# Decoding the signs of 64-bit weights with a Prelu activation, taking arithmetic off GpSimd, and a list ordered anew

## The chip, the cores and the metric

One Trainium2 chip, one of its cores. The metric is the device time of the whole program in microseconds (us), median over runs. The engines are TensorE (PE in the profile, PEld for its weight loads), VectorE (DVE), ScalarE (ACT), GpSimd (POOL) and SyncE (SP), which issues the transfers.

## What is computed

Attention with a learned bias on positions, followed by a two-layer feed-forward block on all tokens (4 batches x 576 positions, 8 heads of 64, model width 512, hidden width 2048):

```python
scores = scale * np.matmul(q, k.transpose(0, 1, 3, 2))
x = (psi_rel / psi_i)[..., None]
h = np.maximum(x @ w1 + b1, 0.0)
bias = h @ w2
scores = scores + bias.transpose(2, 0, 1)[None, :, :, :]
scores = scores - np.max(scores, axis=-1, keepdims=True)
attn = np.exp(scores)
attn = attn / (np.sum(attn, axis=-1, keepdims=True) + 1e-09)
return np.matmul(attn, v).astype(np.float32)
...
x = np.ascontiguousarray(attn_out.transpose(0, 2, 1, 3)).reshape(B * S, H * D)
...
h = x @ w_in
g = h - np.tanh(h)
return (g @ w_out).astype(np.float32)
```

The two weight matrices arrive as 64-bit floats (512x2048 and 2048x512), everything else as 32-bit floats.

## The kernel before, in words

All matrix products run in 16-bit types with every operand split into a high and a low part ("h" and "l", line 403 makes the low one by a subtraction), and three or four products are summed for one.

The program has these steps. Every one is an operation in a list; buffers are named by step.

- Bias: 36 groups of 16 positions. Four ReLU passes (`hg`, 128x576, line 448 on ScalarE or 450 on VectorE), a product with `w2` (`pb`, line 460), a scaled copy out (`bo`, line 469 or 470), and a store to a table in device memory (`bias_d`). The tables `bt` are loaded from there.
- Keys and values: 16 tiles `kv` (128x1152), loaded (`kvst`), narrowed to the high part (line 384 or 385), low part by line 529, and a small rearrangement on GpSimd (lines 536 to 538).
- Weights: 16 chunks `wi` and 16 chunks `wo` of 128x512 (function `weight_chunk`). Each chunk is loaded as pairs of 32-bit words and turned into a 32-bit float: line 489 shifts the low word right by 29, line 494 puts the sign bit of the high word into it, line 384, 385 or 387 multiplies the high word by 2^-111 as a float, line 502 shifts it left by 3 and joins the low word. Then it is narrowed (`win_hi`, `wout_h`) and the low part subtracted (`win_lo`, `wout_l`).
- Attention: 10 blocks (group of two batches, 128 or 64 query rows), in each four pairs of heads. Scores (`ps`, line 588), bias and row minimum (line 602, VectorE), exponential (line 616, ScalarE), reciprocal (623, 624), high part (384, ScalarE), low part (632, VectorE), a transposing transfer (`pt`, line 642, SyncE), product with the values (`px`, line 664), copies `xt` (394, 682).
- Feed-forward, some way behind the attention: `ph` (line 703), tanh (715), h - tanh(h) (720), high part `gh` (384), low part `gl` (402 or 403), `po` (line 730), copies `ot` (394, 395) and the store.

The order is not written by hand. `Plan.order` is a list scheduler that runs through the program once with a duration per operation (`c_mm`, `c_dve`, `c_act` and so on), a latency from each engine to the next (`LAT`), a modelled transfer queue, and a priority per operation (a formula plus a correction from the table `ADJ`). At each moment each free engine takes the ready operation with the best priority. An operation may name several engines (`narrow`, `minus`, `WAYS`); it goes to the one that is done first by weighted load. What comes out is a fixed order on every engine; on the chip each engine takes its own list strictly from the top, and waits by semaphores.

Of the kernel before, what the change touches and what calls it, by code (L numbers as in the profile page):

```python
# [61 lines left out]
class Op:  # L62
    __slots__ = ("alts", "eng", "cost", "fn", "prio", "deps", "outs", "bufs", "start", "end", "left", "idx", "ready", "port")
# [5 lines left out]
class Plan:  # L69
    LAT = {"pe": 190.0, "dve": 200.0, "act": 60.0, "pool": 60.0, "dma": 0.0}  # L70
# [52 lines left out]
    def op(self, eng, cost=None, fn=None, r=(), w=(), prio=0.0, psum=False):  # L123
# [5 lines left out]
        o.port = {e for e, c, _ in alts if e == "pool" and not isinstance(c, tuple) or e == "dve" and not psum}  # L129
# [29 lines left out]
    def order(self):  # L159
# [17 lines left out]
        while done < len(self.ops):  # L177
            moved = False
            claims = {} if loose else self.claimed(cand, now, slots, limit)
            for e in free:  # L180
# [3 lines left out]
                for o in cand[e]:  # L184
                    if o.ready > now or port > now and e in o.port:
                        continue
                    if best is not None and (o.prio, o.idx) >= (best.prio, best.idx):
                        continue
                    if len(o.alts) > 1:
                        mine = now + self.load(e, o.alts[e][0])  # L190
                        if any(
                            max(free[x], now, port if x in o.port else 0.0) + self.load(x, a[0]) < mine
                            for x, a in o.alts.items()
                            if x != e
                        ):
                            continue
# [23 lines left out]
                if isinstance(o.cost, tuple):  # L220
                    issue, move, after, hold = o.cost
                    if e == "dma":
                        hw = max(hw, now) + issue
                        begin = max(hw + 650.0, xfer)
                    else:
                        begin = max(now + SWDGE_HOLD + 650.0, xfer)
# [75 lines left out]
def kernel(  # L302
# [78 lines left out]
    def narrow(n, out, in_, scale=1.0, ptr=0, kind="moe"):  # L381
# [3 lines left out]
            "pool": ("pool", c_pool(n, ptr), lambda: G.tensor_scalar(  # L385
                out(), in_(), scale() if ptr else scale, 1.0, ALU.mult, ALU.mult)),
# [19 lines left out]
    def move(nbytes, out, in_, r=(), w=(), prio=0.0, part=P, hold=(), soft=False):  # L406
# [10 lines left out]
        c = c_dma(nbytes, part)  # L417
# [16 lines left out]
    def bias_group(t, prio):  # L434
# [5 lines left out]
        for j in range(4):  # L440
# [16 lines left out]
        def mms():  # L457
# [7 lines left out]
        op("pe", 1000, mms, r=[(h, y) for h in hgs for y in range(2)] + ["w2"], w=[pb], prio=prio)  # L465
# [10 lines left out]


    def weight_chunk(src, hi, lo, key, prio):
# [3 lines left out]
        def words(i, dt=F32):  # L482
# [10 lines left out]
            "dve", c_dve2(512),  # L493
            lambda: V.scalar_tensor_tensor(  # L494
# [388 lines left out]
```

## Time and profile before

| what | value |
|---|---|
| runs | 680.49, 682.80 and 682.97 us, median 682.8 |
| the profiled execution | span 679.7 us, first to last instruction; what lies around the span is not recorded, the median of the runs is 3.1 us longer |
| busy: PE, DVE, ACT, POOL | 609.4, 485.8, 422.9, 72.2 us |
| mean granted clock of PE | 0.962 of full speed |
| DMA | 114.24 MB, mean 168 GB/s |
| chain that ended last | PE 77%, DVE 15%, DMA 4%, ACT 2%, issue 2% |

Shares are of the span. PE's busy time counts from the first to the last moment at which a matmul is in flight, so it says when PE had work, not how fast it was. In timelines an operation's recorded time overlaps that of the next on its engine by some 0.09 us, so what an operation costs its engine is read from start to start.

### The profile page before, as it was taken

What the parts mean: (1) busy time and instruction counts of PE and PEld (TensorE: products, weight loads), DVE (VectorE), ACT (ScalarE), POOL (GpSimd) and SP (SyncE); (2) the same over time, 40 slices, a digit from 0 to 9 for tenths busy, and PEclk for the clock granted to TensorE, in tenths of its full rate; (3) what the DMA queues carried; (4) which work ended last, traced back from release to release, by engine and by line L of the source; (5) the groups of instructions that cost most, each with busy time, mean ns of one, the idle gap of its engine ahead of it and who ended that gap; (6) DMA issues with size and microseconds to landing.
All of it is one profiled execution on the core that took longest, in us unless ns stands there. A gap on an engine that the chain in (4) does not pass through costs nothing.

```text
span 679.7 us, 18908 instructions
## 1 busy us (share of the span) xinstructions
PE 609.4 (90%) x8096; PEld 481.8 (71%) x8096; DVE 485.8 (71%) x1001; ACT 422.9 (62%) x778; POOL 72.2 (11%) x98
## 2 busy tenths in 40 slices
PE   1782546986999999999999999999999999999997
PEld 0221224764787778788888888888888888888897
DVE  4999999799877867677777987677687576433231
ACT  4996667588776667566665767565587575432231
POOL 4400022010100100000111502000010000000000
PEclk9887677998999999999999999999999999999999
DMA  8898886886755887599968799777578379240010
GB/s 315 291 327 304 222 235 109 275 220 140 264 101 121 155 241 115 135 238 196 240 151 219 164 199 180 165 182 156 90 150 213 71 144 209 41 92 2 1 33 17
DMA packets 193779, 114.24 MB, mean 168 GB/s; under 512 B 171152, under 2 KB 176416, under 8 KB 193696
## 3 DMA queue, kind: packets, MB, share of 16 engines
q1 hardware_dynamic: 193632, 113.03, 68.4%
q8 instruction: 63, 1.03, 0.6%
q14 instruction: 20, 0.16, 0.1%
q0 software_dynamic: 64, 0.02, 0.1%
HBM read 55.22 MB, written 15.34 MB: 104 GB/s over the span
## 4 chain that ended last, share of the span: by engine, by line
PE 77%; DVE 15%; DMA 4%; ACT 2%; issue 2%; SPq 0%; ACTq 0%; DVEq 0%
PE ph L703 28%; PE po L730 28%; PE ps L588 11%; PE px L664 8%; PE pb L460 3%; DVE hl L632 2%; DVE s L602 2%; DMA bt<-bias_d 2%; DMA kvst<-kv 1%; DVE hg L450 1%; DVE ws_wo L494 1%; DVE ws_wo L502 1%; DVE bo L470 1%; DVE ws_wi L502 1%; DMA ws_wi<-w_in 1%
## 5 line engine op out<-in xcount | busy, mean ns | idle before, releaser
L703 PE MATMUL ph<-xt,win_hi 128*128 128x256 f16 (+1 forms) x1280 | 193.8, 262 | 2.7 <-DVE xt L682 1.6
L730 PE MATMUL po<-gh,wout_l 128*128 128x256 bf16 (+1 forms) x640 | 162.3, 263 | 1.0 <-DVE wout_l L403 1.0
L730 PE MATMUL po<-gh,wout_h 128*128 128x256 bf16 (+1 forms) x640 | 162.7, 263 | 0.0
L730 PE MATMUL po<-gl,wout_h 128*128 128x256 f16 (+1 forms) x640 | 162.3, 263 | 0.1
L703 PE MATMUL ph<-xt,win_lo 128*128 128x256 f16 (+1 forms) x640 | 161.4, 262 | 0.4 <-DVE win_lo L403 0.4
L616 ACT ACTIVATE s<-s,mx 128x576 f32<-128x576 f32 x144 | 110.7, 769 | 70.2 <-DVE mx L602 69.6
L703 PEld LDWEIGHTS <-win_hi 128*128 128x128 f16 x1280 | 116.6, 98 | 22.3 <-issue 11.3
L730 PEld LDWEIGHTS <-wout_h 128*128 128x128 f16 x1280 | 117.9, 98 | 19.6 <-issue 8.2
L632 DVE SCALAR_TENSOR_TENSOR hl<-s,mx,hl 128x576 f16<-128x576 f32 x144 | 118.3, 854 | 9.4 <-ACT hl L384 9.2
L588 PE MATMUL ps<-kv,qq 64*128 64x288 f16 (+1 forms) x1280 | 91.8, 304 | 27.9 <-DVE mx L602 15.3
L602 DVE CUSTOM_DVE_ANT_0 s<-ps,bt 128x576 f32<-128x576 f32 x144 | 105.0, 752 | 16.4 <-PE ps L588 15.1
L384 ACT ACTIVATE hl<-s,mx 128x576 f16<-128x576 f32 x144 | 104.3, 764 | 8.1 <-issue 3.1
L720 DVE SCALAR_TENSOR_TENSOR tt<-tt,ph 128x512 f32<-128x512 f32 x72 | 49.4, 687 | 80.1 <-ACT tt L715 80.0
L715 ACT ACTIVATE tt<-ph 128x512 f32<-128x512 f32 x72 | 42.9, 596 | 89.4 <-PE ph L703 89.0
L460 PE MATMUL pb<-hg,w2s 128*32 128x288 f32 x576 | 68.1, 453 | 33.7 <-ACT hg L448 23.2
L588 PEld LDWEIGHTS <-qq 64*128 64x128 f16 (+1 forms) x1280 | 56.0, 103 | 55.5 <-issue 27.6
L460 PEld LDWEIGHTS pb<-hg,w2s 128*32 128x32 f32 x576 | 23.2, 114 | 70.9 <-ACT hg L448 44.5
L664 PEld LDWEIGHTS <-kv 128*64 128x64 f16 x2400 | 63.5, 112 | 10.2 <-issue 10.0
L664 PE MATMUL px<-pt,kv 128*64 128x128 f16 (+1 forms) x2400 | 69.0, 217 | 0.6 <-DMA pt<-hl 0.6
L703 PEld LDWEIGHTS <-win_lo 128*128 128x128 f16 x640 | 62.6, 98 | 8.1 <-issue 1.8
L730 PEld LDWEIGHTS <-wout_l 128*128 128x128 f16 x640 | 63.0, 98 | 7.2 <-DVE wout_l L403 1.2
L448 ACT ACTIVATE hg<-zt,b1l 128x576 f32<-128x576 f32 x83 | 59.5, 763 | 0.5 <-DVE win_lo L403 0.5
(54 smaller groups left out, 477.5 us busy)
## 6 DMA issues: line engine op xcount, KB each, us to landing
bt<-bias_d SPq DMA_DIRECT2D x32, 576.0 KB, 4.9
bias_d<-bo SPq DMA_DIRECT2D x36, 288.0 KB, 4.0
kvst<-kv SPq DMA_DIRECT2D x16, 576.0 KB, 7.3
ws_wi<-w_in SPq DMA_DIRECT2D x16, 512.0 KB, 6.4
ws_wo<-w_out SPq DMA_DIRECT2D x16, 512.0 KB, 6.4
bt<-bias_d SPq DMA_DIRECT2D x16, 288.0 KB, 6.1
qst<-qF SPq DMA_DIRECT2D x8, 512.0 KB, 4.3
outT<-ot SPq DMA_DIRECT2D x16, 256.0 KB, 4.7
```

The costliest lines, as they stand in the source:

```text
L384: "act": ("act", c_act(n, ptr), lambda: A.activation(out(), in_(), AF.Copy, scale=scale() if ptr else scale)),
L448: lambda to=to, src=src, bs=bs: A.activation(to(), src, AF.Relu, bias=bs, scale=1.0)),
L460: nc.tensor.matmul(pb()[32 * j : 32 * j + 32, x, :HS], w2s, hgs[j // 2]()[:, j % 2, x * HS : x * HS + HS], start=True, stop=True, tile_pos ...
L588: nc.tensor.matmul(pss[j]()[w * e : w * e + w, x, :HS], qq()[dp, a, c0 + w * e : c0 + w * e + w], ks()[dp, y, x * HS : x * HS + HS], start ...
L602: V.tensor_tensor_reduce(s().rearrange("p (x k) -> p x k", x=2), ps()[:, :, :HS], bt()[:, j].rearrange("p (x k) -> p x k", x=2), -0.125 / ...
L616: A.activation(s(), s(), AF.Exp, bias=m()[:, j : j + 1], scale=-1.0, accum_out=m()[:, 2 + j : 3 + j])
L632: V.scalar_tensor_tensor(hl()[:, 1, hs], s(), m()[:, 6 + j : 7 + j], hl()[:, 0, hs], ALU.mult, ALU.subtract)
L664: nc.tensor.matmul(px()[64 * j : 64 * j + 64, w * bb : w * bb + w], kw()[:, y, v : v + 64], pt()[:, NCH * l + c, col : col + w], start=(n ...
L703: nc.tensor.matmul(ph()[:, n * (f - f0) : n * (f - f0) + n], w[:, k, f * P : f * P + P], xs[k]()[:, a, :n], start=(k == 0 and e == 0), sto ...
L715: "act", c_actp(512), lambda ph=ph, tt=tt: A.activation(tt(), ph(), AF.Tanh, scale=1.0 / SH),
L720: lambda ph=ph, tt=tt: V.scalar_tensor_tensor(tt(), tt(), -SH, ph(), ALU.mult, ALU.add),
L730: nc.tensor.matmul(po()[:, d // 2, n * (d % 2) : n * (d % 2) + n], wout[w][:, f, d * P : d * P + P], x()[:, n * (f - f0) : n * (f - f0) + ...
```

## The change

1. In `weight_chunk` the sign step (line 494) and the multiplication after it become one activation: `Prelu` with scale 2^-111 and, for negative words, another factor of 2^32. That factor sets the exponent bit that the shift by 3 moves to the sign's place. The step is ScalarE's alone; the multiplication could go to three engines before.
2. GpSimd loses all arithmetic on tiles (`narrow`, `minus`, the ReLU): narrowing goes to ScalarE or VectorE, subtractions to VectorE. It keeps the rearrangement of `kv`, two small loads and one small multiplication.
3. The durations and latencies of the scheduler are other numbers, the transfer model has another form, and the rule that VectorE and GpSimd exclude each other (`port`) is gone.
4. `ADJ` is another table, with an entry for almost every step. The engines' lists differ throughout.

The lists hold 990 rows for VectorE before and 984 now, for ScalarE 619 and 639, for GpSimd 103 and 60, for SyncE 235 and 232; PE has the same 15186 rows in another order.

```diff
-    LAT = {"pe": 190.0, "dve": 200.0, "act": 60.0, "pool": 60.0, "dma": 0.0}
+    LAT = {"pe": 200.0, "dve": 118.0, "act": 132.0, "pool": 85.0, "dma": 0.0}
...
-                    d.ready = max(d.ready, now + (0.0 if same else lat))
+                    d.ready = max(d.ready, now + (SAME[o.eng] if same else lat))
...
+SAME = {"pe": 0.0, "dve": 60.0, "act": 60.0, "pool": 0.0, "dma": 0.0}
...
 def c_dve2(n, ptr=0):
-    return n * 1.05 + 150.0 + 60.0 * ptr
+    return n * 1.0417 + 70.0 + 60.0 * ptr
...
 def c_act(n, ptr=0):
-    return n * 0.833 + 200.0 + 93.0 * ptr
+    return n * 0.8333 + 105.0 + 82.0 * ptr
...
     def minus(n, out, a, b):
-        return [
-            ("pool", c_pool2(n), lambda: G.tensor_tensor(out(), a(), b(), ALU.subtract)),
-            ("dve", c_dve2(n), lambda: V.tensor_tensor(out(), a(), b(), ALU.subtract)),
-        ]
+        return [("dve", c_dve2(n), lambda: V.tensor_tensor(out(), a(), b(), ALU.subtract))]
...
         op(
-            "dve", c_dve2(512),
-            lambda: V.scalar_tensor_tensor(
-                words(0, U32), words(1, U32), 0x80000000, words(0, U32), ALU.bitwise_and, ALU.bitwise_or
-            ),
-            r=[(st, 1)], w=[(st, 0)], prio=prio,
+            "act", c_act(512) + 40.0,
+            lambda: A.activation(words(1), words(1), AF.Prelu, scale=2.0 ** -111, alpha=2.0 ** 32),
+            w=[(st, 1)], prio=prio,
         )
-        op(narrow(512, lambda: words(1), lambda: words(1), 2.0 ** -111, kind="w"), w=[(st, 1)], prio=prio)
...
-    "kv": ("act", "pool"),
-    "w": ("act", "pool", "dve"),
-    "q": ("act", "pool"),
+    "kv": ("act", "dve"),
+    "w": ("act", "dve"),
+    "q": ("act", "dve"),
...
-ADJ = {"wo60": -2.382, "wo00": 1.592, "wo130": 0.423, "wi21": 0.943,
+ADJ = {"b0": 1.041, "b1": -1.377, "b10": -0.125, "b11": -0.096, "b12": 1.001,
```

Three places show how the lists moved. In a name, the last number tells buffers of one kind apart and means nothing else.

**VectorE, the first weight chunk** (`ws_wi_0`, from its first shift to its low part). Before:

```order
L489 TENSOR_SCALAR ws_wi_0_134<-ws_wi_0_134 128x512
L450 TENSOR_SCALAR hg_192<-zt,b1l 128x576
L494 SCALAR_TENSOR_TENSOR ws_wi_0_134<-ws_wi_0_134 128x512
L450 TENSOR_SCALAR hg_205<-zt,b1l 128x576
L387 TENSOR_SCALAR ws_wi_0_134<-ws_wi_0_134 128x512
L489 TENSOR_SCALAR ws_wi_0_150<-ws_wi_0_150 128x512
L502 SCALAR_TENSOR_TENSOR ws_wi_0_134<-ws_wi_0_134 128x512
L470 TENSOR_SCALAR bo_225<-pb_211,rls 128x576
L387 TENSOR_SCALAR win_hi<-ws_wi_0_134 128x512
L494 SCALAR_TENSOR_TENSOR ws_wi_0_150<-ws_wi_0_150 128x512
L403 TENSOR_TENSOR win_lo<-ws_wi_0_134,win_hi 128x512
```

Now:

```order
L477 TENSOR_SCALAR ws_wi_0_137<-ws_wi_0_137 128x512
L440 TENSOR_SCALAR hg_195<-zt,b1l 128x576
L458 TENSOR_SCALAR bo_201<-pb_183,rls 128x576
L487 SCALAR_TENSOR_TENSOR ws_wi_0_137<-ws_wi_0_137 128x512
L440 TENSOR_SCALAR hg_209<-zt,b1l 128x576
L440 TENSOR_SCALAR hg_222<-zt,b1l 128x576 x2
L394 TENSOR_TENSOR win_lo<-ws_wi_0_137,win_hi 128x512
```

The sign step (L494) and the scaling (L387) between shift (L489, now L477) and join (L502, now L487) are gone from VectorE, and the chunk's narrowing (`win_hi`) has moved to ScalarE here.

**ScalarE, at the same chunks** (among the ReLU passes `hg` and the copies `bo` of the bias groups). Before:

```order
L469 ACTIVATE bo_208<-pb_195,rls 128x576
L448 ACTIVATE hg_223<-zt,b1l 128x576 x2
L448 ACTIVATE hg_232<-zt,b1l 128x576 x2
L384 ACTIVATE ws_wi_0_150<-ws_wi_0_150 128x512
L448 ACTIVATE hg_251<-zt,b1l 128x576
L469 ACTIVATE bo_255<-pb_241,rls 128x576
L384 ACTIVATE win_hi<-ws_wi_0_150 128x512
```

Now:

```order
L438 ACTIVATE hg_159<-zt,b1l 128x576
L482 ACTIVATE ws_wi_0_137<-ws_wi_0_137 128x512
L438 ACTIVATE hg_195<-zt,b1l 128x576
L438 ACTIVATE hg_199<-zt,b1l 128x576 x2
L438 ACTIVATE hg_209<-zt,b1l 128x576
L379 ACTIVATE win_hi<-ws_wi_0_137 128x512
L482 ACTIVATE ws_wi_0_157<-ws_wi_0_157 128x512
```

The Prelu (L482) stands in ScalarE's list for each chunk, ahead of the join on VectorE, and the narrowing behind it.

**VectorE, just ahead of the first bias-and-minimum of the third attention block** (the row `s_1_0_0_0`; `tt` and `gl` belong to the feed-forward of the second block, `ot` to the first block's output). Before:

```order
L502 SCALAR_TENSOR_TENSOR ws_wo_0_1853<-ws_wo_0_1853 128x512
L450 TENSOR_SCALAR hg_2250<-zt,b1l 128x576
L682 SCALAR_TENSOR_TENSOR xt_0_3_2237<-px_3_2145,xt_0_3_2237 128x256
L470 TENSOR_SCALAR bo_2256<-pb_2239,rls 128x576
L450 TENSOR_SCALAR hg_2284<-zt,b1l 128x576
L450 TENSOR_SCALAR hg_2289<-zt,b1l 128x576 x2
L403 TENSOR_TENSOR qq_2_2208<-qst_2_2209,qq_2_2208 128x1024
L720 SCALAR_TENSOR_TENSOR tt_0_2304<-tt_0_2304,ph_0_2258 128x512
L450 TENSOR_SCALAR hg_2360<-zt,b1l 128x576 x2
L403 TENSOR_TENSOR gl_0_2366<-tt_0_2304,gh_0_2358 128x512
L395 TENSOR_SCALAR ot_1_2388<-po_1454 128x256
L602 ISA s_1_0_0_0_2418,mx_1_0_0_2419<-ps_0_1_0_0_2368,bt_1_0_2212 128x576
```

Now:

```order
L487 SCALAR_TENSOR_TENSOR ws_wo_0_2085<-ws_wo_0_2085 128x512
L705 SCALAR_TENSOR_TENSOR tt_0_2259<-tt_0_2259,ph_0_2190 128x512
L394 TENSOR_TENSOR wout_l<-ws_wo_0_2079,wout_h 128x512
L394 TENSOR_TENSOR wout_l<-ws_wo_0_2085,wout_h 128x512
L394 TENSOR_TENSOR gl_0_2283<-tt_0_2259,gh_0_2269 128x512
L705 SCALAR_TENSOR_TENSOR tt_2_2281<-tt_2_2281,ph_2_2227 128x512
L440 TENSOR_SCALAR hg_2337<-zt,b1l 128x576 x2
L394 TENSOR_TENSOR gl_2_2345<-tt_2_2281,gh_2_2339 128x512
L440 TENSOR_SCALAR hg_2343<-zt,b1l 128x576
L440 TENSOR_SCALAR hg_2348<-zt,b1l 128x576
L587 ISA s_1_0_0_0_2400,mx_1_0_0_2401<-ps_0_1_0_0_2350,bt_1_0_2252 128x576
```

Ahead of this row stand 316 rows before and 290 now. The last weight chunks stand closer to it, and the second hidden group of that feed-forward (`tt_2`, `gl_2`) has come ahead of it.

## Rows read from the trace of the kernel before

**Rows 1.** Six stretches: length, busy PE, PEld, DVE, ACT, POOL (instructions), PEclk, DMA share, GB/s

```profile
0.00:12.00 12.00, 0.00 (x0) 0.00 (x0) 2.62 (x3) 2.65 (x3) 3.43 (x9) 1.00 0.77 274
12.00:62.00 50.00, 31.96 (x192) 9.67 (x192) 48.68 (x87) 43.30 (x62) 12.16 (x24) 0.89 0.94 331
62.00:120.00 58.00, 31.54 (x474) 18.19 (x475) 54.96 (x116) 39.49 (x74) 9.83 (x9) 0.68 0.75 187
120.00:184.60 64.60, 55.29 (x911) 41.96 (x911) 57.26 (x119) 49.10 (x85) 8.25 (x9) 0.97 0.80 230
184.60:610.00 425.40, 425.40 (x5552) 351.58 (x5553) 303.66 (x650) 271.83 (x527) 38.53 (x48) 1.00 0.74 159
610.00:680.00 70.00, 65.24 (x980) 60.39 (x974) 18.67 (x30) 16.52 (x30) 0.00 (x0) 0.99 0.05 14
```

**Rows 2.** Waits of PE over the whole run: us in total, times, longest

```profile
PE pb L460 <- ACT hg L448: 23.2, 12, 13.7
PE ps L588 <- DVE mx L602: 15.3, 7, 4.7
PE ps L588 <- ACT qq L384: 9.6, 1, 9.6
```

**Rows 3.** Waits of PE from 184.6 us to the end, all there are

```profile
PE ph L703 <- DVE tt L720: 0.4, 1, 0.4
```

**Rows 4.** Timeline of DVE (start, us): first bias-and-minimum of the third attention block

```profile
184.61 0.76 DVE L602 CUSTOM_DVE_ANT_0 s<-ps,bt 128x576 f32<-128x576 f32 x1 [0.24 <-PE ps L588]
```

**Rows 5.** Timeline of DVE, 166 to 172 us

```profile
166.80 0.94 DVE L450 TENSOR_SCALAR hg<-zt,b1l 128x576 f32<-128x576 f32 x2
167.66 0.45 DVE L387 TENSOR_SCALAR wout_h<-ws_wo 128x512 f16<-128x512 f32 x1
168.02 0.45 DVE L489 TENSOR_SCALAR ws_wo<-ws_wo 128x512 uint32<-128x512 uint32 x1
168.36 0.70 DVE L403 TENSOR_TENSOR wout_l<-ws_wo,wout_h 128x512 f16<-128x512 f32 x1
168.99 0.67 DVE L494 SCALAR_TENSOR_TENSOR ws_wo<-ws_wo 128x512 uint32<-128x512 uint32 x1
169.59 1.53 DVE L470 TENSOR_SCALAR bo<-pb,rls 128x576 f32<-128x576 f32 x2
171.04 0.67 DVE L502 SCALAR_TENSOR_TENSOR ws_wo<-ws_wo 128x512 uint32<-128x512 uint32 x1
```

**Rows 6.** Chain of waits in order of time: one feed-forward group, one bias group

```profile
191.11 2.62 PE ph L703 x24
210.67 1.11 PE pb L460 x16
```

**Rows 7.** Waits of DVE in the first 180 us

```profile
DVE kv L529 <- POOL kv L385: 3.4, 1, 3.4
DVE ws_wi L502 <- ACT ws_wi L384: 0.6, 1, 0.6
DVE ws_wo L502 <- ACT ws_wo L384: 0.4, 1, 0.4
```

**Rows 8.** DVE in the first 180 us, groups by line: the attention's low part

```profile
L632 DVE SCALAR_TENSOR_TENSOR hl<-s,mx,hl 128x576 f16<-128x576 f32 x24 | 21.0, 913 | 0.0
```

**Rows 9.** The same operation over the whole run: ns min/median/max

```profile
L632 DVE SCALAR_TENSOR_TENSOR hl<-s,mx,hl x144: 797/814/1714, 77.7 to 601.9; 128x576 f16<-128x576 f32 x144
```

**Rows 10.** Timeline of ACT, 60 to 63 us

```profile
61.45 0.68 ACT L384 ACTIVATE ws_wo<-ws_wo 128x512 f32<-128x512 f32 x1
62.04 0.61 ACT L384 ACTIVATE qq<-qst 128x512 f16<-128x512 f32 x1
```

**Rows 11.** ACT in the first 180 us, groups by line

```profile
L384 ACT ACT_TABLE_LOAD x1 | 1.3, 1283 | 0.7 <-PEq L872 0.7
L384 ACT ACTIVATE ws_wi<-ws_wi 128x512 f32<-128x512 f32 x10 | 6.8, 679 | 2.4 <-issue 1.7 <-DVE ws_wi L494 0.6
```

**Rows 12.** POOL from 180 us on, costliest group

```profile
L402 POOL TENSOR_TENSOR gl<-tt,gh 128x512 f16<-128x512 f32 x13 | 16.1, 1238 | 254.9 <-ACT gh L384 254.8
```

More of the change, by code (lines that the diff above doesn't have):

```diff
@@ L62 @@
 class Op:
-    __slots__ = ("alts", "eng", "cost", "fn", "prio", "deps", "outs", "bufs", "start", "end", "left", "idx", "ready", "port")
+    __slots__ = ("alts", "eng", "cost", "fn", "prio", "deps", "outs", "bufs", "start", "end", "left", "idx", "ready")
 SWDGE_HOLD = 1040.0
 class Plan:
-    LAT = {"pe": 190.0, "dve": 200.0, "act": 60.0, "pool": 60.0, "dma": 0.0}
+    LAT = {"pe": 200.0, "dve": 118.0, "act": 132.0, "pool": 85.0, "dma": 0.0}
     def __init__(self):
@@ L121, in claimed, with op @@
         return claims
-    def op(self, eng, cost=None, fn=None, r=(), w=(), prio=0.0, psum=False):
+    def op(self, eng, cost=None, fn=None, r=(), w=(), prio=0.0):
         o = Op()
         alts = eng if isinstance(eng, list) else [(eng, cost, fn)]
-        o.port = {e for e, c, _ in alts if e == "pool" and not isinstance(c, tuple) or e == "dve" and not psum}
         o.alts = {e: (c, f) for e, c, f in alts}
@@ L184, in order @@
                 for o in cand[e]:
-                    if o.ready > now or port > now and e in o.port:
+                    if o.ready > now:
                         continue
@@ L191, in order @@
                         if any(
-                            max(free[x], now, port if x in o.port else 0.0) + self.load(x, a[0]) < mine
+                            max(free[x], now) + self.load(x, a[0]) < mine
                             for x, a in o.alts.items()
@@ L220, in order @@
                 if isinstance(o.cost, tuple):
[L221 to L226, printed above, removed]
+                    issue, lead, move, after, hold = o.cost
+                    begin = max(now + (lead if e == "dma" else SWDGE_HOLD + 650.0), xfer)
                     xfer = begin + move
-                    free[e] = now + SWDGE_HOLD if e == "pool" else max(hw, begin + 200.0) if hold else hw
+                    free[e] = now + (SWDGE_HOLD if e == "pool" else issue)
+                    if hold:
+                        free[e] = max(free[e], begin + 600.0)
                     o.end = xfer + after
@@ L399, in minus, with move @@
     def minus(n, out, a, b):
-        return [
-            ("pool", c_pool2(n), lambda: G.tensor_tensor(out(), a(), b(), ALU.subtract)),
-            ("dve", c_dve2(n), lambda: V.tensor_tensor(out(), a(), b(), ALU.subtract)),
-        ]
-    def move(nbytes, out, in_, r=(), w=(), prio=0.0, part=P, hold=(), soft=False):
+        return [("dve", c_dve2(n), lambda: V.tensor_tensor(out(), a(), b(), ALU.subtract))]
+    def move(nbytes, out, in_, r=(), w=(), prio=0.0, part=P, hold=(), soft=False, store=False):
         def by(q):
@@ L463, in mms @@
                     )
-        op("pe", 1000, mms, r=[(h, y) for h in hgs for y in range(2)] + ["w2"], w=[pb], prio=prio)
+        op("pe", 1110, mms, r=[(h, y) for h in hgs for y in range(2)] + ["w2"], w=[pb], prio=prio)
         src, out = lambda: pb()[:, :, :HS], lambda: bo().rearrange("p (x k) -> p x k", x=2)
@@ L596, in attn_tile @@
         rd = [(qq, 0), (qq, 1), (bt, 0), (bt, 1)] + [(ks, y) for ks in kss for y in range(2)]
-        op("pe", c_mm(HS, 1, 2 * len(terms)) + 190.0, scores, r=rd, w=pss + [(x, "x") for x in rows + [m]], prio=prio)
+        op("pe", c_mm(HS, 2 * len(terms)) + 100.0, scores, r=rd, w=pss + [(x, "x") for x in rows + [m]], prio=prio)
         for j in range(2):
@@ L684, in attn_out @@
             ),
[L685 removed]
+            r=rd + [(xt, 0)], w=[(xt, 1)], prio=prio,
         )
```

60 lines of the change are left out of this document (26 added, 34 removed).

## The prediction

> **What bounds the kernel now.** First the table of busy time by stretch [rows 1]. From 184.6 us to 610 us PE is busy in every microsecond, at the full clock of 2.4 GHz; after that it idles for 4.8 us at the tail. All other idle time of PE lies ahead of 184.6 us: 184.6 - (32.0 + 31.5 + 55.3) = 65.8 us. From 62 to 120 us the granted clock is 0.68, so PE ran for part of that time at its lower level of 1.2 GHz, after idling. The list of PE's waits agrees [rows 2, 3]: it waited for VectorE and ScalarE (ReLU passes, row minima, queries), and after 184.6 us for 0.4 us in all. So the time is the end of the starved start plus PE's own remaining work. What the change is worth is how much earlier PE gets into its unbroken stretch.
>
> I take as mark the first bias-and-minimum of the third attention block, which starts on VectorE at 184.61 us [rows 4]. All weight chunks are ahead of it in both lists. Ahead of it VectorE was busy for 2.6 + 48.7 + 55.0 + 57.3 = 163.5 us and idle for 21.1, of which 9.4 in the first 12 us, where nothing has landed yet. ScalarE was busy for 134.5 and idle for 50.1 [rows 1]. VectorE is the fuller engine of the start; its list is what I count.
>
> **The change, part by part.** Prices are from start to start [rows 5]: a two-input pass over 128x512 costs VectorE 0.60 us (168.99 to 169.59), a shift 0.34 (168.02 to 168.36), a narrowing 0.36 (167.66 to 168.02), a ReLU pass 0.43 (two in 0.86), a copy `bo` 0.73 (two in 1.45). Between the list before and the list now, ahead of the mark:
>
> - The 32 sign steps go: 32 x 0.60 = -19.2.
> - 11 of the 32 scalings were VectorE's and go; at the price of the shift, which has the same form: 11 x 0.34 = -3.7.
> - 3 copies `bo` fewer, -2.2; 1 copy `ot` fewer, at the shift's price -0.3.
> - From GpSimd come 3 + 4 subtractions of weights, and 2 more `gl` stand ahead of the mark: 9 x 0.60 = +5.4. One more pass of line 720: +0.6.
> - 3 more weight narrowings, +1.1; 3 more ReLU passes, +1.3.
> - 3 narrowings of `kv` (1152 columns) and 2 of queries (1024) are new to VectorE. No row shows them there. Below lies twice the shift of 512 columns, 0.68; above twice the two-input pass, 1.2. I take 0.68, the single-input form. The first `kv` takes the place of a wait of 3.4 us for GpSimd [rows 7] and costs nothing; 4 x 0.68 = +2.7, at most +4.8.
>
> Sum: -25.4 + 11.1 = **-14.3 us** of VectorE's list ahead of the mark.
>
> *GpSimd beside VectorE.* The attention's low part took 913 ns on average in the start [rows 8] and 814 at the median of the run, up to 1714 [rows 9]. I put the 24 x 0.1 us down to GpSimd's passes beside it: **-2.4**. Bounds: 0, if it was something else, and the rule below.
>
> *PE's share ahead of the mark.* One feed-forward group more (2.62 us) and one bias group fewer (1.11) [rows 6] are done by then: **-1.5** of work that remains after it.
>
> *What is given back.* A wait is added: each join on VectorE waits for a Prelu on ScalarE, where 16 chunks waited so far (the other 16 were scaled by VectorE itself or GpSimd). Behind the waiting join everything else of VectorE queues, row minima among it, and for those PE waits. For the 16 the waits of that kind came to 0.6 + 0.4 us [rows 7]. ScalarE also gets fuller. A pass over 512 columns costs it 0.59 us (61.45 to 62.04) [rows 10]; its list gains 19 such passes (16 Prelus, 3 others), +11.2, and loses net 5 of 576 columns, 2 of 1152 and 1 of 1024 and gains one small copy, by width together some -7 (an estimate from 0.59): about +4.3. So 139 us of work would stand in about 168, 83% where it was 73%. Prelu itself has no row; the multiplication on the same tile took ScalarE 679 ns [rows 11], and I take that; were it as long again (0.59 more for each of 32) ScalarE would stand at 94% and take the bound. One table load at the start is all the program has, as before [rows 11]. Lower bound of the loss: none, upper: 16 x 0.6 = 9.6, a whole pass of waiting for each added hand-over. I take **+4**, nearer to the waits seen.
>
> Sum: -14.3 - 2.4 - 1.5 + 4 = **-14.2 us** on the mark relative to PE's work. After the mark nothing of it is lost by my count. What moves to VectorE there (12 `gl`, 3 `kv`, 4 queries, one more query's low part: some 13 us) is hidden under PE: VectorE was busy for 303.7 of 425.4 us, 71% [rows 1], and comes to 74%. If that cover fails, see the second rival. Transfers are the same in number and size; SyncE's three rows fewer are merged neighbours. The tail is unchanged.
>
> 679.7 - 14.2 = 665.5 us of span. The median of the runs is 3.1 us above the profiled span; the same on top gives 682.8 - 14.2 = **668.6 us**.
>
> **Two rules beside the rows.** The excess above is 2.4 us, while GpSimd was busy for 9.8 + 8.3 = 18.1 us between 62 us and the mark [rows 1]. The Trainium skill (SBUF: State Buffer, "Who interferes with whom") says that GpSimd and a VectorE pass with two inputs in SBUF, or in a two-port mode, exclude each other for a whole instruction. By it all 18.1 us could have been taken from VectorE, and the sum would be -29.9. The rows bear out a tenth of that; it is the last rival. A rule against the change is in the same skill (ScalarE: Activation LUTs, "Rules for kernel authors"): multiplications and the like belong on VectorE. In direction the rows agree, 0.34 us there against 0.59 on ScalarE. By that rule the 11 scalings were better left where they are, and the sum without their 3.7 would be -10.5. I hold to the fuller engine's list, because ScalarE had 50 us to spare [rows 1].
>
> **The rivals.**
>
> *The start is held by transfers.* From 12 to 62 us the 16 DMA engines were busy for 94% [rows 1], and in the new list some 6 to 7 us of VectorE's saving lie ahead of the first scores (14 sign steps and 5 scalings fewer, 2 subtractions, 4 ReLU passes and 5 narrowings more, 3 `bo` fewer). The same bytes have to land; 47 us of transfers in 50 leave 3. If these 6.5 us are not to be had, the gain is 7.7: **675 us**. For it: PE's first wait for queries of 9.6 us [rows 2] hangs on a transfer. Against: later stretches have DMA shares of 0.75 to 0.80, so weights may come later without harm.
>
> *PE starves in the middle (slower).* In the unbroken stretch each of some 64 hidden groups needs tanh, difference, high part and low part before PE's next product. Thirteen of these low parts were GpSimd's [rows 12]; now all queue on VectorE, in a list that was fitted to shorter durations and so has less slack, behind attention passes of 0.7 to 0.8 us each. If each group makes PE wait for 0.4 us, the one such wait that the trace shows [rows 3], it costs 64 x 0.4 = 25.6: 668.6 + 25.6 = **694 us**. It decides from 14.2 / 64 = 0.22 us a group on. Against: GpSimd's subtraction took 1.24 us [rows 12], twice VectorE's, and PE still did not wait.
>
> *More than that.* Fitted to durations near the rows (its two-input pass is 603 ns, that of before 688, against 0.60 measured), the list may also take waits out of the 11.7 us that VectorE idled between 12 us and the mark, and the denser PE may keep its clock: nothing given back and 5 us more, -23: **659 us**.
>
> *GpSimd's passes stopped VectorE for their whole length*, all 18.1 us of them [rows 1] in place of the 2.4 counted: -14.2 - 15.7, 682.8 - 29.9 = **653 us**. For it: the longest low part, 1714 ns, twice the median [rows 9]. Against: the average of the start is only 99 ns above it [rows 8].
>
> **How the numbers follow.** A measurement of this kernel can tell about 0.5% from no change, 3.4 us: faster is below 679.4, slower above 686.2. Forecast, 662 to 674 us: 0.55. Held by transfers, or hand-overs near their upper bound, 674 to 682: 0.19, of which 0.06 above 679.4. Starved middle: 0.10, of which 0.02 within the bound. More than that, 655 to 662: 0.12. Exclusion, below 655: 0.04. So faster 0.55 + 0.13 + 0.12 + 0.04 = 0.84, same 0.08, slower 0.08. The range from 655 to 682 leaves out the starved middle and the exclusion, 0.14.
>
> **What would show it.** Right: PE's unbroken stretch starts 13 to 17 us earlier, VectorE's busy time ahead of the mark is near 147 us, its low part of the attention comes to about 0.81 us in the start, the waits of joins for Prelu stay below 5 us, Prelu takes about 0.68 us. Wrong: PE waits after the mark (starved middle), a DMA share near 1.0 up to the first scores with those hardly earlier (transfers), ScalarE with next to no idle time in the start, or Prelu much longer than the multiplication.

## The result, and the profile after

| | before | after |
|---|---|---|
| median of 4 runs each | 682.20 us (680.49 to 682.97) | 663.11 us (662.18 to 665.79) |
| ratio, with its 95% interval | | 0.9731 [0.9705, 0.9757] |
| span of the profiled execution | 679.7 us | 662.1 us |
| mark (third attention block on VectorE) | 184.61 us | 167.35 us |
| from the mark to the end of the span | 495.1 us | 494.8 us |

The change made the kernel 19.1 us faster; 14.2 were forecast. The profiled executions differ by less, 17.6 us of span, in part since that of the change took 663.94 us, 0.8 above its median. Of the 17.6 us, 17.26 lie ahead of the mark. One run of experiment 5 took 3079 us and is counted nowhere. Busy time by stretch after (length; busy us of PE, PEld, DVE, ACT, POOL; granted clock; DMA share; GB/s), beside [rows 1]:

```profile
0.00:12.00 12.00, 0.00 (x0) 0.00 (x0) 3.72 (x4) 3.00 (x3) 2.52 (x10) 1.00 0.79 275
12.00:62.00 50.00, 30.66 (x208) 10.32 (x208) 45.66 (x82) 45.18 (x69) 10.97 (x21) 0.84 0.95 331
62.00:120.00 58.00, 44.37 (x734) 30.51 (x735) 51.92 (x119) 47.69 (x92) 0.00 (x0) 0.69 1.05 229
120.00:167.35 47.35, 39.47 (x647) 31.00 (x645) 44.70 (x93) 40.78 (x73) 0.00 (x0) 0.93 0.91 249
167.35:600.00 432.65, 431.85 (x5695) 356.40 (x5695) 311.39 (x675) 279.19 (x538) 8.02 (x24) 1.00 0.73 158
```

Ahead of the mark VectorE is busy for 3.72 + 45.66 + 51.92 + 44.70 = 146.0 us, 17.5 less than before, and idle for 21.35 (21.1 before). ScalarE stands at 136.65 of 167.35 us, 82%. PE idles for 52.9 us there, 65.8 before. (A DMA share above 1, as from 62 to 120 us, says that the share is a rough measure.)

A second cut shows where in the start the time went. The first bias-and-minimum of the first block starts at 69.66 us before and at 65.56 now. The same view cut there and at the mark, of the kernel before:

```profile
0.00:69.66 69.66, 34.31 (x224) 10.97 (x225) 58.95 (x103) 51.19 (x72) 15.59 (x32) 0.87 0.89 309
69.66:184.61 114.95, 84.49 (x1353) 58.87 (x1353) 104.56 (x221) 83.34 (x151) 18.08 (x18) 0.86 0.78 209
```

and of the change:

```profile
0.00:65.56 65.56, 31.83 (x224) 11.04 (x225) 52.95 (x91) 51.74 (x77) 13.50 (x31) 0.85 0.92 323
65.56:167.35 101.79, 82.66 (x1361) 60.79 (x1361) 93.06 (x205) 84.91 (x158) 0.00 (x0) 0.81 0.99 233
```

Up to the first scores 6.0 us of VectorE's work went, but only 4.1 us of time: transfers were nearly full there before (0.89) and are now (0.92). From there to the mark 11.5 us of work went and 13.2 us of time, and the DMA share rose from 0.78 to 0.99. The granted clock of PE did not gain: 0.87 and 0.86 in the two stretches before, 0.85 and 0.81 now.

Waits of PE after, over the whole run (us in total, times, longest), beside [rows 2]:

```profile
PE pb L448 <- ACT hg L438: 23.7, 10, 13.3
PE ps L573 <- DVE qq L394: 4.8, 1, 4.8
...
PE ps L573 <- DVE mx L587: 4.0, 7, 1.0
PE pb L448 <- DVE mx L587: 2.3, 2, 1.5
```

The scores' waits for row minima (`mx`) fell from 15.3 to 4.0 us, that for the first queries from 9.6 to 4.8. A wait of 4.8 us of line 688 for a narrowing of weights (`win_hi`) is new. From the mark on there are two waits, beside one in [rows 3]:

```profile
PE ps L573 <- DVE mx L587: 0.4, 1, 0.4
PE ph L688 <- DVE tt L705: 0.4, 1, 0.4
```

Waits of VectorE up to the mark, beside [rows 7]:

```profile
DVE ws_wi L477 <- DMA ws_wi<-w_in: 2.7, 2, 1.8
...
DVE ws_wo L477 <- DMA ws_wo<-w_out: 1.1, 1, 1.1
...
DVE ws_wi L487 <- ACT ws_wi L482: 0.2, 1, 0.2
```

and of ScalarE in the first 180 us:

```profile
ACT ws_wo L482 <- DMA ws_wo<-w_out: 3.4, 2, 2.1
ACT ws_wi L482 <- DMA ws_wi<-w_in: 3.0, 3, 1.9
```

A join (line 487) waits for a Prelu once, for 0.2 us. Shift and Prelu wait in all for 2.7 + 1.1 + 3.4 + 3.0 = 10.2 us for weights to land; before, the lists of waits have one of that kind, of 0.4 us on VectorE.

Groups of instructions of ScalarE up to the mark, by form (busy, mean ns), beside [rows 11]:

```profile
L482 ACT ACTIVATE ws_wi<-ws_wi 128x512 f32<-128x512 f32 x16 | 10.8, 690 | 3.0 <-DMA ws_wi<-w_in 3.0
L482 ACT ACTIVATE ws_wo<-ws_wo 128x512 f32<-128x512 f32 x16 | 10.6, 679 | 3.4 <-DMA ws_wo<-w_out 3.4
```

and of VectorE, beside [rows 8]:

```profile
L617 DVE SCALAR_TENSOR_TENSOR hl<-s,mx,hl 128x576 f16<-128x576 f32 x24 | 18.6, 814 | 1.8 <-ACT hl L379 1.7
...
L380 DVE TENSOR_SCALAR kv<-kvst 128x1152 f16<-128x1152 f32 x3 | 2.4, 812 | 1.7 <-DMA kvst<-kv 1.7
...
L380 DVE TENSOR_SCALAR qq<-qst 128x1024 f16<-128x1024 f32 x2 | 1.4, 695 | 0.0
```

Prelu costs what the multiplication cost. The low part takes 814 ns where it took 913, and over the whole run its longest is 820 ns where [rows 9] has 1714.

### The profile page after: what moved, and what is told of

Same layout as the page of the kernel before. It is cut to its first block, busy times and chain, and to the rows that moved or that the text cites. A ratio compares the mean times of both kernels' runs of the same rounds, so it can differ in the third digit from the quotient of the medians.

```text
span 662.1 us, 18824 instructions
## 1 busy us (share of the span) xinstructions
PE 604.5 (91%) x8096; PEld 482.3 (73%) x8096; DVE 473.4 (72%) x994; ACT 429.6 (65%) x796; POOL 21.5 (3%) x55
## 4 chain that ended last, share of the span: by engine, by line
PE 83%; DMA 6%; DVE 5%; ACT 4%; issue 1%; SPq 1%; ACTq 0%; DVEq 0%
PE ph L688 29%; PE po L715 28%; PE ps L573 12%; PE px L649 10%; PE pb L448 4%; DMA ws_wo<-w_out 2%; DMA kvst<-kv 2%; DVE s L587 1%; ACT hg L438 1%; DMA ws_wi<-w_in 1%; DVE hl L617 1%; DVE ws_wi L487 1%; ACT hl L379 1%; SPq L403 1%; DVE win_lo L394 0%
## 5 line engine op out<-in xcount | busy, mean ns | idle before, releaser
L688 PE MATMUL ph<-xt,win_lo 128*128 128x256 f16 (+1 forms) x640 | 163.2, 264 | 0.5 <-DVE win_lo L394 0.5
L688 PEld LDWEIGHTS <-win_hi 128*128 128x128 f16 x1280 | 118.2, 99 | 26.0 <-issue 9.8
L617 DVE SCALAR_TENSOR_TENSOR hl<-s,mx,hl 128x576 f16<-128x576 f32 x144 | 112.3, 814 | 10.6 <-ACT hl L379 10.5
L573 PE MATMUL ps<-kv,qq 64*128 64x288 f16 (+1 forms) x1280 | 91.8, 303 | 14.3 <-DVE qq L394 4.8
L448 PE MATMUL pb<-hg,w2s 128*32 128x288 f32 x576 | 61.3, 461 | 32.5 <-ACT hg L438 23.7
L448 PEld LDWEIGHTS pb<-hg,w2s 128*32 128x32 f32 x576 | 21.4, 117 | 65.0 <-ACT hg L438 36.3
L379 ACT ACTIVATE gh<-tt 128x512 bf16<-128x512 f32 x72 | 45.1, 626 | 32.3 <-DVE tt L705 32.2
```

Source lines behind the costliest of these rows:

```text
L379: "act": ("act", c_act(n, ptr), lambda: A.activation(out(), in_(), AF.Copy, scale=scale() if ptr else scale)),
L448: nc.tensor.matmul(pb()[32 * j : 32 * j + 32, x, :HS], w2s, hgs[j // 2]()[:, j % 2, x * HS : x * HS + HS], start=True, stop=True, tile_pos ...
L573: nc.tensor.matmul(pss[j]()[w * e : w * e + w, x, :HS], qq()[dp, a, c0 + w * e : c0 + w * e + w], ks()[dp, y, x * HS : x * HS + HS], start ...
L617: V.scalar_tensor_tensor(hl()[:, 1, hs], s(), m()[:, 6 + j : 7 + j], hl()[:, 0, hs], ALU.mult, ALU.subtract)
L688: nc.tensor.matmul(ph()[:, n * (f - f0) : n * (f - f0) + n], w[:, k, f * P : f * P + P], xs[k]()[:, a, :n], start=(k == 0 and e == 0), sto ...
```

## The experiments

Each ran beside the kernel before on its own chip, whose medians were 682.45 to 682.69 us. Differences to the change are to its 663.1 us.

**1. Prelu in the old list.** The list of before, row for row: the sign step issues nothing, and each scaling, wherever it stood, is issued as the Prelu on ScalarE.

```diff
-            lambda: V.scalar_tensor_tensor(words(0, U32), words(1, U32), 0x80000000, ...
+            lambda: None,
...
+            [(e, c, lambda: A.activation(words(1), words(1), AF.Prelu, scale=2.0 ** -111, alpha=2.0 ** 32))
+             for e, c, _ in narrow(512, lambda: words(1), lambda: words(1), 2.0 ** -111, kind="w")],
```

> The list of before, row for row, with the sign step left out and the Prelu on ScalarE wherever the scaling stood. Theory (the gain is the work that VectorE's list loses ahead of the mark): 32 x 0.60 + 11 x 0.34 = 22.9 us less on VectorE, 16 more passes of 0.59 on ScalarE; the order was not made for it, so 15 to 23 us faster than before, 659 to 667 us. Rival (the gain is the newly fitted order): within 4 us of before, 678 to 683 us.

Measured 676.67 us, ratio 0.9917 [0.9895, 0.9939]. The work is worth 6.0 us there, so neither theory holds as it stood.

**2. Prelu, and no GpSimd arithmetic, in the old list.** On top of 1:

```diff
-            "pool": ("pool", c_pool(n, ptr), lambda: G.tensor_scalar(out(), in_(), ..., 1.0, ALU.mult, ALU.mult)),
+            "pool": ("pool", c_pool(n, ptr), lambda: V.tensor_scalar(out(), in_(), ..., None, ALU.mult)),
...
-            ("pool", c_pool2(n), lambda: G.tensor_tensor(out(), a(), b(), ALU.subtract)),
+            ("pool", c_pool2(n), lambda: V.tensor_tensor(out(), a(), b(), ALU.subtract)),
```

> The list of before, row for row, with both edits of the work but not the new order: Prelu on ScalarE for sign step and scaling, and every scaling and subtraction that GpSimd did is issued on VectorE at its own place. Theory (the order is what turns the shed work into time): leaving GpSimd idle gives VectorE back some 4 us of lengthened passes in the start, but its 3 + 4 + 6 passes ahead of the mark cost about as much; 673 to 678 us, within 4 of the Prelu alone (676.7), and some 11 us short of the change. Rival (GpSimd's interference was the bigger part of the gain): below 669 us.

Measured 679.52 us, ratio 0.9958 [0.9941, 0.9976], 2.9 above the first: within the 4 us that the theory allowed beside the Prelu alone, but 1.5 above its range and 16.4 above the change. The rival falls. Here the work is the change's and the list the old one. Its start, in the same two stretches (first scores at 67.77 us, mark at 182.09):

```profile
0.00:67.77 67.77, 33.04 (x224) 10.43 (x225) 49.65 (x82) 54.14 (x79) 11.39 (x31) 0.90 0.88 311
67.77:182.09 114.32, 85.29 (x1353) 59.62 (x1353) 96.54 (x212) 87.95 (x160) 0.00 (x0) 0.82 0.80 213
```

VectorE is busy for 146.2 us ahead of the mark, against 146.0 in the change, and yet the mark comes 14.7 us later: the engine idles for 35.9 us instead of 21.35. Where, VectorE's waits up to 182 us tell:

```profile
DVE ws_wi L504 <- ACT ws_wi L498: 5.5, 8, 1.4
...
DVE ws_wo L504 <- ACT ws_wo L498: 3.6, 7, 1.3
DVE mx L625 <- ACT s L618: 3.5, 7, 1.0
DVE bo L470 <- PE pb L460: 2.4, 3, 1.2
DVE win_lo L403 <- ACT win_hi L384: 2.3, 4, 0.8
```

The joins wait for the Prelu 15 times, 9.1 us in all. The old list puts the Prelu where a scaling stood, close ahead of its join; the list of the change has it early enough that one such wait is left, of 0.2 us. From the end of a Prelu to the start of its join (paired in their order, `wi` and `wo` apart) the two traces have medians of 0.05 us here and 1.1 us in the change.

**3. The sign step back in the new list.** The list of the change, row for row, with a multiplication in place of the Prelu and the sign step issued on VectorE right ahead of each join:

```diff
-            lambda: A.activation(words(1), words(1), AF.Prelu, scale=2.0 ** -111, alpha=2.0 ** 32),
+            lambda: A.activation(words(1), words(1), AF.Copy, scale=2.0 ** -111),
...
+                V.scalar_tensor_tensor(words(0, U32), words(1, U32), 0x80000000, words(0, U32), ...),
                 V.scalar_tensor_tensor(words(1, U32), words(1, U32), 3, words(0, U32), ...),
```

> The list of the change, row for row, with a plain scaling in the Prelu's place and the sign step back on VectorE, right ahead of each join. Theory: 32 x 0.60 = 19.2 us more ahead of the mark, 14 to 19 us slower than the change, 677 to 682 us. Rival (order): within 4 us of the change, 662 to 667 us.

Measured 679.28 us, ratio 0.9953 [0.9939, 0.9967]: 16.2 us slower than the change for 19.2 us of passes, the mark at 183.53 us. As the theory had it. The two stretches of its start (first scores at 72.42 us):

```profile
0.00:72.42 72.42, 36.69 (x224) 12.57 (x225) 63.35 (x107) 52.49 (x78) 11.23 (x31) 0.79 0.87 296
72.42:183.53 111.11, 84.97 (x1361) 62.78 (x1361) 103.19 (x221) 85.23 (x157) 0.00 (x0) 0.79 0.83 214
```

16 of the 32 passes stand ahead of the first scores (107 rows for 91), and these come 6.9 us later, though the same transfers had to land. So in the new list the 32 passes count for five sixths of their length; in the old list, they and the 11 scalings together for 6.0 us.

**4. Without the priority corrections.** `ADJ = {}` in the change, so that the planner orders by the formulas alone.

> The change with an empty table of corrections to the priorities, so the planner orders by its formula alone; all work is the same. Theory: VectorE has the same 146 us ahead of the mark, and the corrections are worth only the waits between engines: 663 to 671 us. Rival (order): most of the gain goes, 675 us or more.

Measured 671.16 us, ratio 0.9842 [0.9815, 0.9868], at the upper end of the theory's range: 8.1 us of the gain are the fitted corrections. PE's waits over the whole run:

```profile
PE pb L448 <- DVE mx L587: 15.2, 6, 6.0
PE ps L573 <- DVE mx L587: 12.2, 7, 4.5
```

27.4 us of waits for row minima, against 4.0 + 2.3 in the change; all other waits of PE together are some 13 us shorter than there. What the fit buys is, on balance, minima that come in time.

**5. The old planner with the Prelu.** Before, ordered by its own durations and corrections, with the Prelu as an operation of ScalarE.

```diff
+            "act", c_act(512),
+            lambda: A.activation(words(1), words(1), AF.Prelu, scale=2.0 ** -111, alpha=2.0 ** 32),
+            w=[(st, 1)], prio=prio,
```

> Before, ordered anew by its own rules (old durations, old priority corrections) with the Prelu as an operation of ScalarE of the old duration; GpSimd keeps its arithmetic. Theory: any order made with the Prelu in view uses VectorE's shed work, and only the fit of durations and corrections is missing, which the run without corrections priced at 8 us; 667 to 674 us. Rival (the fit is all, an unfitted order loses what the Prelu gives): 677 us or more.

Four runs took 685.05 to 689.95 us; the ratio is 1.0072 [1.0043, 1.0101], some 687.5 us by it: slower than before, and the rival's time holds. PE's three largest waits for VectorE:

```profile
PE ps L585 <- DVE mx L599: 21.2, 14, 5.9
PE pb L460 <- DVE hg L450: 8.5, 4, 6.1
PE pb L460 <- DVE mx L599: 5.0, 2, 4.1
```

The scores wait 21.2 us for row minima where they waited 15.3 [rows 2]. That the corrections, fitted to another set of operations, do this harm is likely but not shown: the old durations stood beside them, and no run of this planner left the corrections out.

**6. Eight more transfers in the start of the change.** Each of the first 8 weight chunks is also copied to a spare place in device memory.

```diff
+            issue()
+            if len(spare) < 8:
+                nc.sync.dma_start(spare_d[len(spare)], src)
```

> The change with each of the first 8 weight chunks also copied to a spare place in DRAM, on the queue that loads the weights: 8 x 512 KB more transfers ahead of the first scores, nothing else changed. Theory (the start is bound by VectorE's and ScalarE's lists): weights wait, but the lists are long enough behind; at most 5 us, up to 668 us. Rival (the start is held by transfers): 512 KB at the about 330 GB/s of the start is 1.6 us, 8 of them push the first scores by 12.7 us; 674 us or more.

**7. The same in the kernel before.**

> The kernel before with the same eight extra 512 KB copies that cost the change 9.4 us. Theory (the bound of the start moved: before, VectorE's list held it, and transfers had slack, with a DMA share of 0.75 to 0.80 from 62 us to the mark): clearly less, 0 to 6 us, 683 to 689 us. Rival (the transfers held the start of both alike): 8 to 11 us, 691 us or more.

The change came to 672.52 us, ratio 0.984 [0.9791, 0.9888], 9.4 us slower, with runs from 667.79 to 675.58, so that the 9.4 is good to some 3 us; the profile is of a run of 674.1. The kernel before came to 691.77 us, ratio 1.0143 [1.0123, 1.0163], 9.3 us slower. The theories of both runs fall. In 7 the rival's time came; in 6 the time lies 1.5 us below the rival's, which had 1.6 us for each copy. The bound didn't move from VectorE's list to the transfers: more transfers cost both kernels the same. The stretches of the change with the copies (first scores at 74.72 us, mark at 177.38):

```profile
0.00:74.72 74.72, 32.26 (x224) 11.36 (x225) 53.32 (x91) 52.47 (x77) 11.05 (x31) 0.76 0.96 340
74.72:177.38 102.66, 80.80 (x1361) 60.17 (x1361) 92.83 (x206) 85.47 (x159) 0.00 (x0) 0.84 0.97 233
```

and of before with them (78.36 and 195.04):

```profile
0.00:78.36 78.36, 35.65 (x224) 12.33 (x225) 59.25 (x103) 51.27 (x72) 15.54 (x32) 0.81 0.93 328
78.36:195.04 116.68, 85.81 (x1353) 60.57 (x1353) 104.61 (x221) 83.22 (x151) 17.43 (x18) 0.82 0.80 205
```

Nearly the whole delay is there at the first scores (+9.2 and +8.7 us, 1.1 for each 512 KB), and nothing later makes it good (+0.9 and +1.7 in the second stretch). That transfers alone hold the start is not shown by this: 16 more passes on VectorE moved the first scores by 6.9 us (experiment 3). Both count.

**8. The low part `gl` twice on VectorE**, in each of the 72 feed-forward groups of the change.

```diff
+            low = minus(512, gl, tt, gh)
+            op([(e, c, lambda f=f: (f(), f())) for e, c, f in low], r=[tt, gh], w=[gl], prio=top)
```

> The change with the feed-forward's low part (the last VectorE pass ahead of PE's next product) done twice in each of the 72 groups: 0.60 us more on VectorE in each, 6 of them ahead of the mark. Theory (the middle has slack, PE's 71 to 74% VectorE cover holds): only the passes ahead of the mark cost, 3.6 us; 663 to 668 us. Rival (the hidden groups' chain is at its limit, so that each 0.60 us shows): 66 x 0.4 to 0.6 us; 690 us or more.

Measured 676.03 us, ratio 0.99 [0.9878, 0.9922]: 12.9 us slower, between the two. The mark stays where it was (167.29 us), but not because the six extra passes ahead of it were free: the first scores came at 64.30 us, 1.26 earlier than in the profile of the change, with nothing changed ahead of them, and from there to the mark it took 1.2 us longer. Most of the loss is behind it. PE's waits there:

```profile
PE ps L573 <- DVE mx L587: 6.7, 14, 1.0
PE pb L448 <- DVE mx L587: 0.9, 1, 0.9
PE po L716 <- DVE gl L394: 0.8, 1, 0.8
PE ph L688 <- DVE tt L705: 0.4, 1, 0.4
```

The 66 groups behind the mark cost 673.2 - 167.29 - 494.75 = 11.2 us, 0.17 us for each pass of 0.60. So the middle has slack for most of a pass, but not for all of it.

**9. Half of the weights' low parts on GpSimd.** The change, planned as it is, with the subtraction of 16 of the 32 chunks issued there.

```diff
+        if (key[1] + key[2]) % 2:
+            low = [(low[0][0], low[0][1], lambda: G.tensor_tensor(lo(), words(1), hi(), ALU.subtract))]
```

> The change with the low-part subtraction of 16 of the 32 weight chunks on GpSimd (ordered again by the same planner with the same priorities). Theory with the small price for GpSimd beside VectorE (2.4 us for 18.1 us of GpSimd): VectorE loses 9.6 us and is held up by some 2.7 us for 20.5 us of GpSimd; 2 to 7 us faster than the change, 656 to 661 us, or no gain if the slower low part is waited for. Rival (GpSimd stops VectorE for its whole length): 20.5 - 9.6 = 11 us slower, 674 us, with long VectorE passes beside each GpSimd pass.

Measured 666.86 us, ratio 0.9776 [0.9751, 0.98], 3.8 slower, though VectorE has 16 passes (9.6 us) less to do. GpSimd's two groups ahead of the mark:

```profile
L495 POOL TENSOR_TENSOR wout_l<-ws_wo,wout_h 128x512 f16<-128x512 f32 x8 | 13.0, 1628 | 51.6 <-ACT wout_h L379 41.6 <-DVE wout_h L380 10.0
L495 POOL TENSOR_TENSOR win_lo<-ws_wi,win_hi 128x512 f16<-128x512 f32 x8 | 10.5, 1322 | 65.5 <-DVE win_hi L380 39.3 <-DVE mx L611 11.3 <-ACT win_hi L379 10.2
```

Against the mean of the same form in the change, VectorE's passes up to the mark came out 11.0 us longer in all, for 23.5 us of GpSimd's. The theory fell, and so did the rival (674 us): what came back was half of GpSimd's time, neither a tenth nor all of it.

**10. The change, fitted again.** The planner's price of a load is raised to what the start shows, and the corrections are fitted anew, by random trials, judged by the end time that the planner computes.

```diff
     move = nbytes / 412.0 * (128.0 / part)
+    if not store:
+        move *= 412.0 / 350.0
...
+ADJ = {"b32": -355.00262, "b33": -377.65764, "b34": -288.22063, ...
```

> The work of the change, ordered anew: the planner's price of a load is raised from 412 to 350 bytes per ns (the start moved 331 GB/s at a DMA share of 0.95), and the priority corrections are fitted again to that. Theory (the change's order reckons with weights landing too early, which shows as 10.2 us of waits of VectorE and ScalarE for weight transfers ahead of the mark): an order that reckons with it gets part of them back, 654 to 660 us. Rival (the transfers themselves hold the start, whatever the order): 661 to 665 us.

**11. The sign step, fitted.** The planner of 10, with the sign step and the scaling of before as operations, GpSimd still without arithmetic.

> As the refitted change, but with the sign step and the scaling of before in place of the Prelu (32 passes more on VectorE, the scaling on ScalarE or VectorE), and an order fitted to that by the same procedure. Theory (the Prelu's 19.2 us of VectorE's list are worth their share once both orders are fitted): 5 to 14 us above the refitted change. Rival (the fit is the whole gain, the Prelu only moves work): within 3 us of the refitted change.

**12. GpSimd kept, fitted.** The planner of 10, with `"pool"` again among the engines of `minus` and `w`, and in VectorE's place for `kv` and `q`, as before the change.

> As the refitted change, but GpSimd may again take subtractions, narrowings of keys, values and queries, and weight scalings, as in before, with an order fitted to that by the same procedure. Theory (about half of GpSimd's busy time comes back as longer VectorE passes, 9 to 11 us over the whole run in earlier runs, of which 4 to 5 ahead of the mark): 1 to 6 us above the refitted change. Rival (the longer passes lie under PE and the freed VectorE list counts): equal to the refitted change or up to 4 us below it.

Measured: 661.23 us for 10, ratio 0.9698 [0.9677, 0.9718]; 673.90 us for 11, 0.9877 [0.9846, 0.9908]; 682.94 us for 12, 1.0014 [0.9998, 1.003]. The first is the fastest kernel here, by 1.9 us, with intervals that still overlap; the rival of 10 holds, since better knowledge of the transfers bought little. Each list being fitted by the same procedure, the Prelu is worth 12.7 us of the 19.2 that leave VectorE's list, as the theory of 11 had it; how far two such fits of one set of operations lie apart was not tried. And with GpSimd's arithmetic back nothing of the gain is left, 21.7 us where the theory had 1 to 6 and the rival none. The timeline of VectorE in 12 shows what happens there (start, us):

```profile
18.48 0.68 DVE L498 SCALAR_TENSOR_TENSOR ws_wi<-ws_wi 128x512 uint32<-128x512 uint32 x1
19.08 1.38 DVE L488 TENSOR_SCALAR ws_wi<-ws_wi 128x512 uint32<-128x512 uint32 x1
20.38 1.42 DVE L451 TENSOR_SCALAR hg<-zt,b1l 128x576 f32<-128x576 f32 x1
...
22.31 0.51 DVE L451 TENSOR_SCALAR hg<-zt,b1l 128x576 f32<-128x576 f32 x1
...
23.08 0.42 DVE L488 TENSOR_SCALAR ws_wi<-ws_wi 128x512 uint32<-128x512 uint32 x1
```

and that of GpSimd:

```profile
18.63 1.54 POOL L403 TENSOR_TENSOR win_lo<-ws_wi,win_hi 128x512 f16<-128x512 f32 x1 [1.30 <-DVE win_hi L388]
20.13 1.34 POOL L403 TENSOR_TENSOR win_lo<-ws_wi,win_hi 128x512 f16<-128x512 f32 x1
```

Two subtractions run there, to 20.17 and to 21.47 us. The shift at 19.08 takes 1.38 us (0.42 at 23.08), so it ends 0.29 us behind the first; the ReLU at 20.38 takes 1.42 (0.51 at 22.31) and ends 0.33 behind the second. So, as far as GpSimd's rough spans tell, each waited for a subtraction to end. Up to the mark GpSimd did 58.2 us of arithmetic in 12, and VectorE's passes were 24.2 us longer than in the change. The planner knows nothing of that, and its durations for GpSimd (1.16 us for a subtraction of 512 columns) are short of the rows (1.4 to 1.5 us), so the 21.7 us price such a fit, not every use of GpSimd. Whether an order that keeps the two engines' passes apart would gain by GpSimd was not tried.

The medians side by side, in us (a dash: not run):

| list | sign step, GpSimd used | Prelu, GpSimd used | sign step, GpSimd idle | Prelu, GpSimd idle |
|---|---|---|---|---|
| that of before | 682.2 | 676.7 | - | 679.5 |
| that of the change | - | - | 679.3 | 663.1 |
| fitted to the work | - | 682.9 | 673.9 | 661.2 |

## Why the prediction was right, and which of its steps were not

*What bounds the kernel.* Right: PE's work behind the mark was the same (490.6 us before, 490.0 now), and all but 0.35 us of the gain lies ahead of it, inside the 13 to 17 us that the text named as the sign of being right, but for 0.3 us.

*The total.* The time came 5.5 us below the forecast and 1.1 above the lower bound of its range. 3.4 us of the 5.5 are the terms below. The other 2.1 are the step from span to median: 3.1 us were taken from before, and for the change it is 1.0. The change's profiled run lies 1.8 us above its own span, so that step held over 1 us of the scatter between runs, which no term stood for.

*VectorE's list and GpSimd beside it*, -14.3 and -2.4. Busy time ahead of the mark fell by 17.5, to 146.0 where 147 was named. The low part's 0.1 us for each of 24 passes came as counted, to 0.814; the small additions ahead of the reciprocal, ReLU and joins had been lengthened too, by 1.7 us together. The new narrowings were a little off: from recorded means less the 0.09 us of overlap, 0.72 us for `kv` and 0.61 for queries, where 0.68 was taken for both.

*PE's share*, -1.5. Measured: 8 matmuls fewer behind the mark (6520 before, 6512 now), as the 24 less 16 of the two groups have it, but only 0.6 us less of work, of which 0.35 reached the end. Where the other 0.9 us went is open.

*What is given back*, +4, bounds 0 and 9.6. This is the term that failed: VectorE's idle time is 21.35 us where it was 21.1, so in sum next to nothing was given back. ScalarE did fill up as forecast (136.65 us where 139 was written), Prelu took 0.68 to 0.69, but the joins waited for 0.2 us. The upper bound was real in the other list, 9.1 us in experiment 2. Which of the two it would be stood in the order of the new list, in how far ahead of its join the Prelu is issued, and I took a middle value instead. That the sum of the idle time stayed is also luck: 3.8 us of waits for weights to land came in (2.7 + 1.1), which the term did not have, and the wait of 3.4 us for GpSimd's `kv` [rows 7] went. By terms, the sum missed by -0.8 for busy time, -3.75 for what was given back, and +1.15 for PE's share: -3.4, from 14.2 to 17.6.

*The reason.* The sum counted the length of VectorE's list and took its idle time as given. That gave the right size, but is not the whole reason: with the same length in the old order (experiment 2) the mark comes 14.7 us later, and the sign step alone put back costs 16.2 us. The Prelu alone gains 6.0 us in the old list (3.1 with GpSimd idle), the new list without the Prelu 3.4 (GpSimd idle and all scalings on ScalarE there), all together 19.1. In the old order the passes taken out left holes: VectorE then waited for ScalarE instead, 9.1 us of it at the joins (experiment 2).

*The rivals.* "The start is held by transfers" was half right: of the 6 to 7 us that the text counted ahead of the first scores, 4.1 were had, waits for landing weights came up (10.2 us), and each 512 KB more cost 1.1 us, as it did before. But the 2.4 us lost there were more than made good behind it, where the DMA share still had room (0.78); the text had the right mechanism in the right stretch and let it hold for the total. "More than that" (659) was right that the idle time gives nothing back, and wrong that waits and PE's clock would add 5 us: the idle time did not shrink, and the granted clock ahead of the mark was 0.83 where it had been 0.86. "PE starves in the middle" did not come, and experiment 8 shows the margin: with 0.60 us more in each group 11.2 us are lost behind the mark, 0.17 for each, so that the dozen low parts taken over from GpSimd could cost little.

"GpSimd's passes stop VectorE for their whole length" was given 0.04 on the evidence of one operation's mean. The Trainium skill (SBUF — State Buffer, "Who interferes with whom") says that whichever engine is first gets the shared ports for its whole instruction, and the timeline of experiment 12 agrees for the two passes shown: 1.38 us for a shift of 0.42. What it makes of a start is another matter: against the means of the change, VectorE's passes ahead of the mark were longer by 3.6 us for 19.2 us of GpSimd's arithmetic in the kernel before, 11.0 for 23.5 in experiment 9, 24.2 for 58.2 in experiment 12. So the -2.4 that I took was near for the old list, and the price of GpSimd in another list can't be read from it. The other rule that the prediction weighed (ScalarE: Activation LUTs, "Rules for kernel authors", in the Trainium skill) speaks for leaving the 11 scalings on VectorE; that was not tried apart.

## What to carry to other kernels

A pass taken off the fullest engine is worth most of its length only in an order made for its absence (here 12.7 and 16.2 of 19.2 us, and 6.0 of 22.9 in the old order): price the work and the order together, and try the work in the old order, and the old work in the new one, before believing either. Where a wait is added, read in the new list how far ahead of the waiting instruction its producer is issued; that settles a term whose bounds lie 9.6 us apart. Do not take a helper engine for free: GpSimd's arithmetic beside VectorE gave back a fifth to a half of its busy time as longer VectorE passes.

## What the runs showed of the hardware that was not expected

- A single-input VectorE pass that starts beside a GpSimd subtraction can take three times as long (shift 0.42 to 1.38 us, ReLU 0.51 to 1.42); over a start the lengthening was 0.19, 0.47 and 0.42 of GpSimd's arithmetic in three orders (before, experiments 9 and 12).
- Prelu with a slope of 2^32 on 128x512 32-bit floats took ScalarE 679 to 690 ns, as the plain multiplication (679), with no table load beyond the one at the start.
- In the start an extra device-memory copy of 512 KB moved the first scores by 1.1 us and the end by 1.2 in either kernel, though no list of a compute engine was touched.
